# A tuned attention and feed-forward kernel: its first phase issued in another hand-listed order

## The chip, the cores and the metric

The kernel runs on one core of one Trainium2 chip. The metric is the device time of one execution in microseconds (us). Three runs of the kernel before gave 1009.29, 1008.87 and 1005.37 us; their median is 1008.87 us.

## The reference

The reference is a pooled attention whose output goes through a gated feed-forward layer. It is float32 throughout.

```python
k_p = k.reshape(B, H, Sp, 8, D).mean(axis=3)          # B=8, H=8, S=576, D=64, Sp=72
v_p = v.reshape(B, H, Sp, 8, D).mean(axis=3)
scores = q @ k_p.T / sqrt(D)
attn = softmax(scores)
x = (attn @ v_p) as 4608 tokens x 512
xn = x / sqrt(mean(x * x) + 1e-6) * rms_g
out = (silu(xn @ w_gate) * (xn @ w_val)) @ w_out      # 512 -> 1536 -> 512
```

## The kernel before, in words

The kernel has nine token blocks of 512 tokens. A first phase (`ORDER`, run by `first_phase`) computes the attention of batches 0 and 1, converts all weights from float64 words to pairs of float32r parts, and runs the feed-forward layer of block 0. A later phase (`LATER`) does the rest and is not changed. Within a phase the whole order of work is written out by hand: `ORDER` is a list of steps, `run` calls them one after another, and each engine executes its own instructions in just that order. An engine that waits therefore holds everything that stands behind it in its own list. GpSimd (POOL) and the queue of SyncE (SP), which issues all transfers, are kept in order in the same way.

A step is a letter with indices (base 36); after a colon stand the PSUM banks that it takes. The ones that matter here:

- For batch b and head pair p: `k`, `q`, `v` load (L361, L369, L380, on SP); `K` and `V` pool by eight on VectorE (L389, L398); `S` makes the scores on TensorE (L441). For each head h: `M` row maxima on VectorE (L407, L408), `E` exponentials on ScalarE (L419), `R` inverse sums on VectorE (L425, L426), `N` normalises on GpSimd (L431, tile prob for batch 1, main for batch 0). `T` transposes on TensorE (L501), `C` and `D` copy the result out by VectorE or ScalarE (L507, L509), `A` multiplies by the pooled v (L523), `Y`, `X` copy (L545), `Z`, `Q` square on ScalarE (L550, L560, L567), `J` joins the squares on GpSimd (L574, L576), `P` sums them on TensorE (L616), `p` adds two parts on VectorE (L621), `r` is a square root on ScalarE (L628), `s` its inverse on VectorE (L631), `B` spreads it on TensorE (L640), `I` scales block 0 on VectorE (L1008), `H` scales the rest.
- For weight chunk n of 26: `l` loads it (L290, SP), `a` takes the magnitude on ScalarE (L301), `b`, `c`, `d` put the bits together on VectorE (L305, L309, L313), `h` rounds on ScalarE (L327), `w` takes the remainder on VectorE (L331). Chunks 0 and 1 belong to slice 0 of the first layer, 2 to slice 1, 3 to slice 0 of the second layer, then alternately the first layer and the second.
- For slice f of 12 of block 0: `x`, `y` round the input and take its remainder (L1013 ScalarE, L1018 VectorE), `g` and `e` are the two products of the first layer, 12 matmuls each (L1029, tile psg), `G` is the silu on ScalarE (L1036), `F` the product with e on VectorE (L1041), `i` and `j` round and take the remainder (L1051, L1059), `o` is the product of the second layer, 12 matmuls (L1073, tile po). All `g` share bank 2 and all `e` bank 3.
- `z` with a count: so many products of the identity with itself, which nothing reads (`warm`, L1145). Each appears in the trace as two matmul records.

`ORDER` ends with the rounding of the next block's input (`t`) and the two last products `oa`, `ob`. Two more lists give the buffers out of which tiles are taken in turn: `OUTS` (two buffers, for the magnitudes of the second layer's chunks among others) and `STAGES` (four buffers, for loads and squares).

The lines that place the steps in engines are these:

```python
N=lambda b, p, h: s_norm(b, p, h, G), T=s_pt,
g=lambda f: mm1(0, f, 0), e=lambda f: mm1(0, f, 1), G=lambda f: gate(0, f), F=lambda f: val(0, f),
z=warm, t=lambda c: (x_hi(1, c), x_lo(1, c)))
nc.sync.dma_start(gcol, gain)
run(ORDER, 1, steps)
```

Of the kernel before, what the change touches and what calls it, by code (L numbers as in the profile page):

```python
# [49 lines left out]


ORDER = """
zg:0 k01 q00 k00 v00 K00 S00:01 K01 q01 v01 z1:7 S01:45 q02 k02 v03 v02 k03 q03 l3 M000 E000 l1 l0 V00 M010 M011 E011
l2 l5 k10 q10 R000 N000 M001 E001 K02 zf:7 S02:06 E010 T000:5 R011 N011 T011:1 V03 M020 E020 K03 z1:7 S03:32 R001 M021
E021 N001 T002:0 C011 M030 R020 N020 E030 C000 T001:1 C001 D002 M031 E031 R030 R021 N021 z4:7 T020:4 C020 V02 N030
R010 N010 z1:7 A001:0 Z01 Y001 R031 N031 A000:1 Z00 V01 a1 b1 c1 z1:7 T021:5 T022:0 D022 Y000 D021 a0 b0 T030:4 D030
A020:1 Z20 Y020 T010:0 D010 a2 c0 d0 z2:7 T012:1 C012 d1 A021:0 Z21 T031:4 C031 K10 T032:5 C032 Y021 h1 w1 h0 w0
A010:1 Z10 Y010 A011:0 Z11 l4 S10:46 M100 b2 M101 Y011 a5 b5 c2 A030:5 Z30 A031:0 J02 J01 a3 b3 Z31 z2:2 P01:7 za:2
P03 p X030 E100 R100 c3 E101 R101 N101 d3 r0 s0 zd:2 B00:1 Y031 N100 z2:2 T100:0 v10 V10 a4 b4 k11 K11 I2 l6 q11 v11
D100 I0 I1 I3 a6 b6 z3:2 T102:0 D102 T101:5 D101 B01:4 A100:0 x0 y0 x1 y1 x2 y2 Y100 x3 y3 h3 w3 A101:1 Y101 g0:2 e0:3  # L60
G0 d2 h2 c6 c5 l7 a7 w2 d6 h6 F0 i0 c4 b7 d4 h4 H01 j0 c7 S11:01 M111 d7 g1:2 e1:3 h7 G1 w4 d5 F1 o0:4567 g2:2 Q10 w7
h5 w5 i1 j1 l9 a9 lb l8 la ld a8 w6 b9 c9 ab bb M110 cb b8 d9 db G2 E110 R110 N110 o1 e2:3 g3:2 c8 F2 h9 E111 R111 V11
k12 w9 K12 d8 v12 lc q12 aa i2 j2 ba T110:0 D110 ad bd h8 w8 N111 T111:1 D111 ca cd da T112:0 D112 G3 e3:3 o2 g4:2 F3
dd ac bc cc hb hd wd wb A110:1 A111:0 Y110 i3 j3 Y111 e4:3 lf af bf V12 cf G4 ha wa o3 g5:2 lh le k13 F4 ae i4 dc j4
o4 v13 df ah bh be ce K13 de ch hc wc e5:3 G5 F5 dh he we lj lg li S12:01 M121 i5 M120 j5 q13 ll lm ag bg hh wh cg dg
hf ai bi wf aj bj cj g6:2 G6 e6:3 F6 o5 dj g7:2 e7:3 E121 R121 N121 E120 al i6 j6 bl hj wj hg Q11 R120 N120 cl J11
T121:0 C121 G7 F7 wg ci di T120:1 D120 T122:0 D122 lk ln ak bk o6 ck dl i7 am j7 A121:1 X121 V13 bm A120:0 Y120 hi wi
hl g8:2 G8 o7 Q12 J12 S13:01 M130 wl M131 dk E130 cm R130 E131 R131 an bn cn hk e8:3 F8 g9:2 dn hn wn i8 j8 N131
T131:0 D131 N130 T130:1 C130 e9:3 o8 T132:0 G9 dm hm D132 F9 i9 wk ga:2 A130:0 wm X130 A131:1 X131 lp ap lo ao bo Q13
j9 bp ea:3 o9 Ga cp dp Fa ia hp k20 v20 K20 ja co do J13 P10:0 r1 s1 gb:2 B10:0 H10 B11:1 Gb ho H11 eb:3 wo oa Fb ib  # L70
jb wp t2 t0 t3 t1 V20 ob q20
"""


# [138 lines left out]
dp7621 dp7631 dp7641 dp7651 do741 de741  # L213
"""
OUTS = """
0101110110010110010101010101010101010101010010101010101010101010101010101010101010101010101010101010101010101010
"""

DEEP = (7,)
# [3 lines left out]
HM = DM // 2  # L223

STAGES = """
0123023102310232131203103213231201233102131221302121032130213231031323132113210302330113003210203210320120323013031201
0130232121023101010231032132102103021302301
"""
EXP_SCALE = 1.0 / (POOL * float(np.sqrt(D)))
# [952 lines left out]
```

## Time and profile before

| what | value |
|---|---|
| median of three runs | 1008.87 us (1005.37 to 1009.29) |
| the profiled execution's own time | 1004.35 us |
| its span, first to last instruction | 1002.6 us |
| TensorE busy | 970.5 us (97%) |
| VectorE busy | 699.2 us (70%) |
| ScalarE busy | 492.8 us (49%) |
| GpSimd busy | 302.6 us (30%) |
| mean granted TensorE clock | 0.995 |

The profile is of one execution. Busy shares are means over the span; the first phase takes its first 176 us, where the shares are others. In the timelines a row gives the start, the duration, the engine, the line, the operation and its tiles, and in brackets the idle time of the engine before it with the work that ended that idle time. Matmul records overlap, so a group of 12 of them shows some 2.9 us in a row of its own and 2.72 us in the chain of waits, which counts from the end of the one before.

### The profile page before, as it was taken

How to read it: one execution, taken by the hardware profiler on the slowest of the kernel's cores; microseconds unless marked ns; L12 is line 12 of the kernel's file. 1: busy time of each engine (PE TensorE's matmuls, PEld its weight loads, DVE VectorE, ACT ScalarE, POOL GpSimd, SP SyncE). 2: the span in 40 equal slices, each digit the busy share in tenths (PEclk: the TensorE clock that was granted, in tenths of full speed). 3: DMA queues.
4: the chain of work that ended last, by engine and by line, in shares of the span. 5: the costliest groups of instructions: out<-in, count | busy, mean ns of one | idle time of the engine just before them, and what ended most of it. 6: DMA issues, size and time to landing. Idle time of an engine off the chain costs nothing.

```text
span 1002.6 us, 14211 instructions
## 1 busy us (share of the span) xinstructions
PE 970.5 (97%) x4832; PEld 764.5 (76%) x4832; DVE 699.2 (70%) x1131; ACT 492.8 (49%) x907; POOL 302.6 (30%) x285
## 2 busy tenths in 40 slices
PE   8996999999999999899999999999999999999998
PEld 7774867767677778787777878777788787888876
DVE  6996987775776857657778788876644655445565
ACT  5874765565556545344665464764222432223232
POOL 2303022376544678300111023155432001113330
PEclk9998999999999999999999999999999999999999
DMA  9534521677867772467777662777676606666665
GB/s 304 167 132 163 211 63 37 219 228 244 248 192 220 222 222 77 158 212 213 221 213 222 192 205 67 226 222 237 204 215 211 220 25 206 193 195 189 187 186 186
DMA packets 130200, 189.40 MB, mean 189 GB/s; under 512 B 10896, under 2 KB 76944, under 8 KB 128848
## 3 DMA queue, kind: packets, MB, share of 16 engines
q1 hardware_dynamic: 130128, 188.49, 61.1%
q8 instruction: 39, 0.64, 0.3%
q14 instruction: 33, 0.27, 0.1%
HBM read 132.22 MB, written 56.23 MB: 188 GB/s over the span
## 4 chain that ended last, share of the span: by engine, by line
PE 77%; DVE 9%; ACT 5%; DMA 3%; POOL 3%; issue 3%; SPq 1%; ACTq 0%; DVEq 0%; POOLq 0%
PE py L829 19%; PE po L1073 18%; PE px L829 14%; PE psg L1029 12%; PE pd L964 6%; PE psx L523 3%; PE pss L441 3%; POOL prob L431 1%; DVE hl L1059 1%; DMA main<-kT 1%; DMA out<-o 1%; DVE xraw L607 1%; ACT prob L419 1%; DVE w L331 1%; DVE act L1041 1%
## 5 line engine op out<-in xcount | busy, mean ns | idle before, releaser
L829 PE MATMUL py<-xp,wp 128*128 128x512 f32 x864 | 222.0, 392 | 0.9 <-DVE u L1137 0.8
L829 PEld LDWEIGHTS py<-xp,wp 128*128 128x128 f32 x864 | 160.6, 188 | 39.1 <-DVE u L1137 4.0
L1029 PE MATMUL psg<-xh,w 128*128 128x512 f32 x576 | 183.1, 400 | 3.5 <-DVE act L1041 3.0
L1073 PE MATMUL po<-w,hh 128*128 128x512 f32 x672 | 174.6, 390 | 0.0
L829 PE MATMUL px<-xp,wp 128*128 128x512 f32 x648 | 166.7, 393 | 2.2 <-ACT act L1132 2.2
L1073 PEld LDWEIGHTS po<-w,hh 128*128 128x128 f32 x672 | 126.0, 188 | 27.4 <-issue 0.8
L829 PEld LDWEIGHTS px<-xp,wp 128*128 128x128 f32 x648 | 120.3, 188 | 32.8 <-ACT act L1132 3.2
L1029 PEld LDWEIGHTS psg<-xh,w 128*128 128x128 f32 x576 | 106.6, 190 | 34.1 <-issue 6.7
L1029 PE MATMUL psg<-xl,w 128*128 128x512 f32 x288 | 112.6, 393 | 0.0
L472 POOL TENSOR_TENSOR prob<-prob,sm 128x360 f32<-128x360 f32 x48 | 40.8, 850 | 231.6 <-DVE sm L468 188.7
L1073 PE MATMUL po<-w,hl 128*128 128x512 f32 x336 | 97.4, 399 | 3.9 <-DVE hl L1059 3.6
L1073 PEld LDWEIGHTS po<-w,hl 128*128 128x128 f32 x336 | 61.2, 188 | 23.5 <-DVE hl L1059 7.5
L1130 ACT COPY hb<-px 128x512 f32<-128x512 f32 x36 | 21.2, 588 | 93.2 <-PE px L829 93.1
L1133 DVE TENSOR_TENSOR u<-u,py 128x512 f32<-128x512 f32 x36 | 24.7, 686 | 59.6 <-PE py L829 59.6
L1135 ACT ACTIVATE hb<-hb 128x512 f32<-128x512 f32 x36 | 22.7, 632 | 83.6 <-DVE hb L1134 83.4
L1029 PEld LDWEIGHTS psg<-xl,w 128*128 128x128 f32 x288 | 54.6, 189 | 12.0
L1059 DVE TENSOR_TENSOR hl<-act,hh 128x512 fp32r<-128x512 f32 x60 | 48.4, 807 | 20.7 <-ACT hh L1051 18.6
L964 PE MATMUL pd<-dp,wq 128*128 128x512 f32 x252 | 61.2, 390 | 0.3 <-DVE dp L937 0.3
L1051 ACT CAST hh<-act 128x512 fp32r<-128x512 f32 x60 | 37.3, 622 | 48.7 <-DVE act L1041 28.8
L964 PEld LDWEIGHTS pd<-dp,wq 128*128 128x128 f32 x252 | 47.2, 188 | 10.5 <-DVE dp L937 0.7
L738 POOL TENSOR_TENSOR wsum<-wsum 128x256 f32<-128x256 f32 x48 | 48.7, 1014 | 1.4
L462 ACT ACT_TABLE_LOAD x38 | 48.8, 1283 | 0.7
(160 smaller groups left out, 1506.0 us busy)
## 6 DMA issues: line engine op xcount, KB each, us to landing
wp<-sum SPq DMA_DIRECT2D x144, 256.0 KB
wp<-blocks SPq DMA_DIRECT2D x108, 256.0 KB
sum<-wt SPq DMA_DIRECT2D x48, 256.0 KB
blocks<-w SPq DMA_DIRECT2D x24, 512.0 KB
wx<-w SPq DMA_DIRECT2D x10, 1024.0 KB
v<-vN SPq DMA_DIRECT2D x32, 288.0 KB
wx<-w SPq DMA_DIRECT2D x16, 512.0 KB
k<-kT SPq DMA_DIRECT2D x28, 288.0 KB
```

The source lines that it names most:

```text
L441: nc.tensor.matmul(s["ps", h][:, t * SP:(t + 1) * SP], s["q"][r, o:o + P], s["pk"][r, :], start=True, stop=True)
L462: nc.scalar.activation(l_pr(h), l_pr(h), AF.Exp, scale=EXP_SCALE)
L472: nc.gpsimd.tensor_tensor(l_pr(h), l_pr(h), sm[:, :, None].broadcast_to([P, len(OFFS2), SP]), ALU.mult)
L523: nc.tensor.matmul(ps[r, :n], s["pv"][:, r], x, start=True, stop=True)
L738: nc.gpsimd.tensor_sub(place(f, y), place(f, a), place(f, b))
L829: nc.tensor.matmul(ps[:, :NB], w[:, a, c, :], x[:, b, c, :], start=j == 0 and not more, stop=j == len(todo) - 1, skip_group_check=more)
L964: nc.tensor.matmul(ps[:, :NB], w[:, a, c * P:(c + 1) * P], x[b], start=g == 0 and j == 0 and not more, stop=g == HF - 1 and j == 2, skip_g ...
L1029: nc.tensor.matmul(ps[:, :NB], w[:, c, cols], x[c], start=(j == 0), stop=(j == len(todo) - 1))
L1051: nc.scalar.copy(a, act_in(i, f))
L1059: eng.tensor_sub(l, act_in(i, f), hh[i, f].bitcast(F32))
L1073: nc.tensor.matmul(po[i, t], x[i, f][:, t * P:(t + 1) * P], w, start=(f == 0 and k == 0), stop=(f == NF - 1 and k == 2))
L1133: u3=lambda i, f: V.tensor_add(u3(i), u2(i), st["Y", i, f, 3]),
```

## The change

The list `ORDER` is replaced by another one. It holds the same steps, each on the same engine and with the same banks; the steps `z` alone differ in their counts. Of these, the first (16 products) stays, and the rest have 46 products where there were 55. Among the moves:

- `E101` stands behind `r0` and `s0`, where it stood before `r0`.
- `A100`, `A101` and `B01` stand behind `g0 e0`, where they stood ahead of `g0`; `V10` and `b4` stand behind `y3`.
- `G2` stands behind `E110` and `E111`, where it stood ahead of both.
- `T111` and `T110` stand behind `e3 o2`; they stood behind `g3`, ahead of `e3`. `N110` and `N111` are issued around `w6 db c8`.
- `A110` and `A111` stand ahead of `o3`, `J11` and `J12` behind `N130`, and `r1` ahead of `Ga`.

`OUTS` and `STAGES` change in a few places to go with it.

```diff
--- before.py
+++ after.py
@@ -50,25 +50,25 @@
 
 
 ORDER = """
-zg:0 k01 q00 k00 v00 K00 S00:01 K01 q01 v01 z1:7 S01:45 q02 k02 v03 v02 k03 q03 l3 M000 E000 l1 l0 V00 M010 M011 E011
-l2 l5 k10 q10 R000 N000 M001 E001 K02 zf:7 S02:06 E010 T000:5 R011 N011 T011:1 V03 M020 E020 K03 z1:7 S03:32 R001 M021
-E021 N001 T002:0 C011 M030 R020 N020 E030 C000 T001:1 C001 D002 M031 E031 R030 R021 N021 z4:7 T020:4 C020 V02 N030
-R010 N010 z1:7 A001:0 Z01 Y001 R031 N031 A000:1 Z00 V01 a1 b1 c1 z1:7 T021:5 T022:0 D022 Y000 D021 a0 b0 T030:4 D030
-A020:1 Z20 Y020 T010:0 D010 a2 c0 d0 z2:7 T012:1 C012 d1 A021:0 Z21 T031:4 C031 K10 T032:5 C032 Y021 h1 w1 h0 w0
-A010:1 Z10 Y010 A011:0 Z11 l4 S10:46 M100 b2 M101 Y011 a5 b5 c2 A030:5 Z30 A031:0 J02 J01 a3 b3 Z31 z2:2 P01:7 za:2
-P03 p X030 E100 R100 c3 E101 R101 N101 d3 r0 s0 zd:2 B00:1 Y031 N100 z2:2 T100:0 v10 V10 a4 b4 k11 K11 I2 l6 q11 v11
-D100 I0 I1 I3 a6 b6 z3:2 T102:0 D102 T101:5 D101 B01:4 A100:0 x0 y0 x1 y1 x2 y2 Y100 x3 y3 h3 w3 A101:1 Y101 g0:2 e0:3
-G0 d2 h2 c6 c5 l7 a7 w2 d6 h6 F0 i0 c4 b7 d4 h4 H01 j0 c7 S11:01 M111 d7 g1:2 e1:3 h7 G1 w4 d5 F1 o0:4567 g2:2 Q10 w7
-h5 w5 i1 j1 l9 a9 lb l8 la ld a8 w6 b9 c9 ab bb M110 cb b8 d9 db G2 E110 R110 N110 o1 e2:3 g3:2 c8 F2 h9 E111 R111 V11
-k12 w9 K12 d8 v12 lc q12 aa i2 j2 ba T110:0 D110 ad bd h8 w8 N111 T111:1 D111 ca cd da T112:0 D112 G3 e3:3 o2 g4:2 F3
-dd ac bc cc hb hd wd wb A110:1 A111:0 Y110 i3 j3 Y111 e4:3 lf af bf V12 cf G4 ha wa o3 g5:2 lh le k13 F4 ae i4 dc j4
-o4 v13 df ah bh be ce K13 de ch hc wc e5:3 G5 F5 dh he we lj lg li S12:01 M121 i5 M120 j5 q13 ll lm ag bg hh wh cg dg
-hf ai bi wf aj bj cj g6:2 G6 e6:3 F6 o5 dj g7:2 e7:3 E121 R121 N121 E120 al i6 j6 bl hj wj hg Q11 R120 N120 cl J11
-T121:0 C121 G7 F7 wg ci di T120:1 D120 T122:0 D122 lk ln ak bk o6 ck dl i7 am j7 A121:1 X121 V13 bm A120:0 Y120 hi wi
-hl g8:2 G8 o7 Q12 J12 S13:01 M130 wl M131 dk E130 cm R130 E131 R131 an bn cn hk e8:3 F8 g9:2 dn hn wn i8 j8 N131
-T131:0 D131 N130 T130:1 C130 e9:3 o8 T132:0 G9 dm hm D132 F9 i9 wk ga:2 A130:0 wm X130 A131:1 X131 lp ap lo ao bo Q13
-j9 bp ea:3 o9 Ga cp dp Fa ia hp k20 v20 K20 ja co do J13 P10:0 r1 s1 gb:2 B10:0 H10 B11:1 Gb ho H11 eb:3 wo oa Fb ib
-jb wp t2 t0 t3 t1 V20 ob q20
+k01 zg:0 q00 k00 K01 v00 q01 v01 q02 k02 v03 K00 V00 S00:01 M000 E000 M001 v02 k03 q03 l3 l1 l0 z1:7 S01:45 M010 M011
+E011 E001 K02 za:7 S02:06 R000 N000 T000:5 R011 N011 T011:1 M020 E020 R001 N001 z3:7 T002:0 V03 K03 S03:32 l2 l5 k10
+M021 C011 E010 R010 N010 R020 N020 M030 T001:1 C001 E021 C000 R021 N021 z4:7 T020:4 V01 V02 D002 A001:0 E030 R030 C020
+M031 Y001 Z01 A000:1 Z00 Y000 a1 b1 z1:7 T022:0 D022 a0 b0 c1 d1 T021:5 D021 T010:0 N030 T030:4 E031 R031 D010 A020:1
+Y020 Z20 c0 d0 D030 z3:7 A021:0 Z21 Y021 T012:1 C012 h1 h0 N031 T031:4 C031 K10 A011:0 Z11 A010:1 Z10 J02 w1 T032:5
+C032 q10 S10:46 M100 l4 v10 k11 l6 Y011 a2 b2 a3 b3 c2 Y010 c3 M101 A030:5 Z30 A031:0 Y031 Z31 J01 z2:2 P01:7 z8:2 P03
+p d3 E100 R100 N100 r0 s0 z9:2 B00:1 E101 z2:2 T100:0 D100 d2 X030 I0 h3 I3 R101 N101 z3:2 T102:0 w0 x0 T101:5 a5 I1
+I2 x1 x2 b5 y0 y1 y2 x3 y3 g0:2 e0:3 V10 a4 b4 D102 D101 A100:0 h2 w2 B01:4 c5 G0 F0 c4 i0 d5 H01 w3 q11 v11 l7 a7 l9
+lb d4 b7 j0 c7 h4 w4 h5 w5 d7 K11 g1:2 e1:3 a6 b6 G1 F1 A101:1 o0:4567 Y100 ab Y101 h7 w7 c6 i1 j1 a9 l8 a8 S11:01
+M111 M110 bb d6 cb E110 b8 R110 N110 h6 w6 db c8 E111 R111 N111 b9 g2:2 G2 o1 e2:3 F2 hb wb d8 V11 la ld k12 v12 i2 lc
+q12 lf ad bd lh j2 cd c9 d9 dd g3:2 G3 e3:3 o2 aa ba F3 h8 w8 V12 K12 ca da T111:1 T110:0 D111 h9 ac bc g4:2 e4:3 hd
+i3 j3 D110 wd T112:0 G4 D112 A110:1 A111:0 w9 F4 ha wa o3 g5:2 cc dc i4 ah af bf j4 o4 e5:3 cf df le k13 v13 lj lg ae
+hf bh wf be ce hc Y111 wc G5 de aj Y110 ag S12:01 ch bj M121 E121 bg M120 F5 cj dh R121 N121 i5 j5 cg he we E120 dg dj
+R120 g6:2 G6 e6:3 o5 g7:2 hj F6 wj i6 j6 hh wh T121:0 C121 li q13 ai ll lm al Q11 am lk bi bl cl dl ci V13 hg N120
+T120:1 D120 T122:0 D122 G7 e7:3 wg o6 g8:2 hl F7 A121:1 A120:0 wl bm cm K13 i7 Q10 j7 o7 ln lp an bn di cn dn ak bk
+X121 ck G8 Y120 S13:01 M130 M131 hi wi E130 R130 dk E131 R131 N131 N130 hk hn dm J11 Q12 J12 e8:3 F8 g9:2 i8 j8 T131:0
+D131 hm wm G9 wn T130:1 lo k20 ap wk C130 bp cp ao dp bo co do T132:0 D132 e9:3 F9 i9 o8 A130:0 X130 A131:1 X131 Q13
+J13 ga:2 ea:3 P10:0 r1 j9 o9 Ga Fa s1 ia gb:2 hp wp ja B10:0 ho wo B11:1 H10 H11 eb:3 oa Gb Fb ib jb t0 t2 t3 t1 K20
+v20 q20 V20 ob
 """
 
 
@@ -213,7 +213,7 @@
 dp7621 dp7631 dp7641 dp7651 do741 de741
 """
 OUTS = """
-0101110110010110010101010101010101010101010010101010101010101010101010101010101010101010101010101010101010101010
+0101010110001010101001010101010101010101010010101010101010101010101010101010101010101010101010101010101010101010
 """
 
 DEEP = (7,)
@@ -223,7 +223,7 @@
 HM = DM // 2
 
 STAGES = """
-0123023102310232131203103213231201233102131221302121032130213231031323132113210302330113003210203210320120323013031201
+0123013210302132021320303213231201233102131221302121032130213231031323132113210302330113003210203210320120323013031201
 0130232121023101010231032132102103021302301
 """
 EXP_SCALE = 1.0 / (POOL * float(np.sqrt(D)))
```

## Rows read from the trace of the kernel before

**Rows 1.** The page: TensorE's granted clock in 40 slices of 25 us

```profile
PEclk9998999999999999999999999999999999999999
```

**Rows 2.** Windows: stretch, its us, busy us of each engine, clock, DMA

```profile
48.24:74.60 26.36, 26.36 (x131) 21.38 (x131) 25.56 (x42) 19.02 (x44) 1.58 (x1) 1.00 0.36 133
...
48.24:176.03 127.79, 115.58 (x571) 91.29 (x570) 107.06 (x163) 78.05 (x164) 23.50 (x11) 0.97 0.34 120
```

**Rows 3.** Timeline of TensorE: transposes that waited for GpSimd

```profile
84.42 1.50 PE L501 MATMUL pst<-ident,prob 128*72 128x128 f32 x6 [9.34 <-POOL prob L431]
...
144.80 0.63 PE L501 MATMUL pst<-ident,prob 128*72 128x128 f32 x4 [1.35 <-POOL prob L431]
146.00 0.63 PE L501 MATMUL pst<-ident,prob 128*72 128x128 f32 x4 [0.56 <-POOL prob L431]
```

**Rows 4.** Timeline of GpSimd in the first phase

```profile
41.22 2.86 POOL L431 TENSOR_TENSOR prob<-prob,mx 128x360 f32<-128x360 f32 x2 [6.60 <-DVE mx L426]
...
74.83 9.54 POOL L431 TENSOR_TENSOR prob<-prob,mx 128x360 f32<-128x360 f32 x1 [0.43 <-DVE mx L426]
121.71 0.79 POOL L431 TENSOR_TENSOR prob<-prob,mx 128x360 f32<-128x360 f32 x1 [37.34 <-ACT wt L301]
...
143.67 2.27 POOL L431 TENSOR_TENSOR prob<-prob,mx 128x360 f32<-128x360 f32 x2 [5.48 <-ACT wt L301]
...
159.35 2.72 POOL L729 TENSOR_TENSOR wsum<-w 128x1024 f32<-128x1024 f32 x1
```

**Rows 5.** Timeline of VectorE, around two of those

```profile
74.60 1.18 DVE L398 TENSOR_REDUCE pv<-v 72x128 f32<-72x1024 f32 x1
...
82.50 1.22 DVE L313 SCALAR_TENSOR_TENSOR wt<-wx,wt 128x1024 uint32<-128x1024 uint32 x1
...
89.42 0.69 DVE L1041 TENSOR_TENSOR act<-act,psg 128x512 f32<-128x512 f32 x1 [5.71 <-PE psg L1029]
90.03 0.69 DVE L313 SCALAR_TENSOR_TENSOR wt<-wx,wt 128x512 uint32<-128x512 uint32 x1
...
159.86 2.76 DVE L313 SCALAR_TENSOR_TENSOR wt<-wx,wt 128x512 uint32<-128x512 uint32 x1
```

**Rows 6.** Windows of 10 us, with the columns of rows 2

```profile
80.00:90.00 10.00, 5.58 (x22) 4.62 (x23) 4.29 (x5) 4.15 (x6) 4.37 (x1) 0.66 0.87 357
```

**Rows 7.** The chain that ended last: start, us, what

```profile
70.60 1.63 ACT prob L419 x10
...
85.92 3.40 PE psg L1029 x12
...
92.04 2.72 PE psg L1029 x12
...
136.52 1.32 PE pss L441 x20
```

**Rows 8.** Timeline of TensorE, up to the first product of block 0

```profile
35.93 2.48 PE L1145 MATMUL warm<-ident 128*128 128x128 f32 x20
...
39.19 3.15 PE L1145 MATMUL warm<-ident 128*128 128x128 f32 x26
42.17 1.22 PE L640 MATMUL psb<-ident,r 116*128 116x116 f32 x10
...
46.12 0.33 PE L640 MATMUL psb<-ident,r 116*128 116x64 f32 x2
46.64 1.67 PE L523 MATMUL psx<-pt,pv 72*64 72x288 f32 x8 [0.19 <-ACT pt L509]
48.24 2.12 PE L1029 MATMUL psg<-xh,w 128*128 128x512 f32 x8
```

**Rows 9.** Timeline of VectorE ahead of that product

```profile
44.02 2.71 DVE L1008 SCALAR_TENSOR_TENSOR xraw<-xraw,gcol,psb 128x512 f32<-128x512 f32 x4
...
47.62 2.55 DVE L1018 TENSOR_TENSOR xl<-xraw,xh 128x512 fp32r<-128x512 f32 x4 [0.30 <-ACT xh L1013]
```

**Rows 10.** Timeline of ScalarE there: the table load of the square root

```profile
38.40 1.28 ACT L628 ACT_TABLE_LOAD   x1
```

## The prediction

> **What bounds the kernel now.** I read the span first: TensorE is busy for most of it, so the question is where in the first phase, which alone changes, TensorE stands still. The windows come next. From the first product of block 0 at 48.24 us to the phase's last product at 176.03 lie 127.79 us, of which TensorE is busy 115.58 and VectorE 107.06 [rows 2]. In the part up to 74.60 TensorE has no idle time at all and VectorE next to none, 25.56 of 26.36 us. So this stretch is bound by TensorE, with VectorE close behind.
>
> Then the timeline of TensorE: of the 12.2 us that it loses, 9.34 are one wait at 84.42, of the transposes T111 for GpSimd; 1.35 and 0.56 are later waits of the same kind [rows 3]. GpSimd's timeline shows what it was: the norm N111 begins at 74.83 and takes 9.54 us [rows 4], where a norm with nothing in its way takes 0.79. VectorE's timeline gives the reason: from 74.60 to 83.72 it runs without a gap, and the norm ends 0.65 us after that run [rows 5]. TensorE stood still meanwhile, with its next product behind T111, and its clock was granted at 0.66 in the window from 80 to 90 us, so for a part of it at 1.2 and not 2.4 GHz [rows 6]. VectorE in turn had to wait 5.71 us afterwards for a product [rows 5]. What stands before 48.24 us is a chain of latencies, where TensorE fills its time with unread products [rows 8].
>
> **The change, part by part.** The work is the same; only its places and 9 products fewer.
>
> *The wait for N111.* In the new list R111 and N111 come some 26 us after the first product, and between the scores S11 and T111 stand g2, o1, e2, g3, e3 and o2. Six groups at 2.72 us [rows 7] are 16.3 us, where g2, o1, e2, g3 gave 10.9. The cover counts from when N111 can begin, and at the latest it is let in at F3, whose operand comes from PSUM and which follows e3; o2 still runs then, for 2.72 us, and a norm takes 0.79. So the wait goes: -9.34. With it goes the slow clock: the product group after it took 3.40 us in the chain, the next like it 2.72 [rows 7], so 0.7, and half again for the transposes: -1.0.
>
> *Ahead of the first product.* The fillers between the last attention products and B00 shrink: 20 and 26 records took 2.48 and 3.15 us [rows 8], and 16 and 18 will take 2.0 and 2.2, together 1.45 less. The square root can follow, because E101 (1.5 us) no longer stands before it on ScalarE. E101 then pays a table load that it did not pay before, 1.28 [rows 10]; its user is T101, not the chain of the root. B00 ended at 43.39, so will at 41.9. VectorE began the four scalings I at 44.02 and ended y3 at 50.17 [rows 9]; V10 and b4 no longer stand before the scalings but after y3, and R101, w0 and b5 come in between, half a microsecond more than stood there. The end of y3, which the first product's last part waits for, comes at about 48.2: -2.0. Bounds: 0, if E101's inverse sum R101 is late, and +5, if N101 is late (below).
>
> *Moved behind it.* A100, A101 and B01 now run behind the first product: 0.33 and 1.67 us [rows 8], 2.0 more that TensorE does after it: +2.0. It was part of the time before 48.24 and its going is in the -2.0 above.
>
> *New waits.* The norms of the last pair keep their waits of 1.35 and 0.56 [rows 3]: S13, e8, g9 and T131 stand as they stood. G2 now stands behind E110, a weight cast and E111. In the last pair the first norm began at 143.67 [rows 4], 5.8 us after the scores' end at 137.84 [rows 7]; with the cast and a second table load it is some 8.5 until G2 ends, and g3 needs its bank. The cover is g2, o1, e2, 8.2 us. Between 0 and +1.5; I take +0.6, for the row of the norm is the nearest. J11 and J12 now run back to back behind N130. A GpSimd operation that has begun keeps VectorE out: a 512-column operation beside the 2.72 us sum of weights took 2.76 us [rows 4, 5] and 0.69 without [rows 5]. The loss was 2.07 for 1024 columns; a join has 576, so 1.2 each by an estimate from those rows. F9 stands behind that run and frees bank 3 for ea. Between 0 and +2.4; I take half, +1.2.
>
> *Queues.* SP: v11 waits until V10 has freed its buffer, and l7, l9 and lb queue behind it; V10 comes later by 6 us, and so do these loads. Their first user a7 stands on ScalarE behind G0 and i0, which wait for g0 and e0: cost 0, and 2 if the load lands after that. GpSimd: only norms and joins, dealt with. The buffers taken in turn: a7 now follows w3's release, but h4 behind it waits for d4 at about that time anyway: 0, at most 1.
>
> *The sum.* -9.34 - 1.0 - 2.0 + 2.0 + 0.6 + 1.2 = -8.5 us. The later phase begins with products of the next block that follow without a gap, so the phase's gain is carried to the end. The profiled execution took 1004.35 us, which gives 995.8. That execution lies 4.5 below the median of the runs; against 1008.87 the forecast is **1000.3 us**.
>
> *A rule against the rows.* Row first: N111 began 0.2 us into V11, a reduction of 1.18 us from 74.60 on, and was not done with it; it was held for the whole run [rows 4, 5]. The Trainium skill ("SBUF — State Buffer", section "Who interferes with whom") says that a reduction never contends with GpSimd, and that whichever operation starts first has the shared ports for its whole length. By that N111 would have begun inside V11 and been done at 75.6; its 9.54 us would have another cause, which another order may cover but does not take away, and the sum would be that of the third rival in place of -8.5. The measurement decides: for the reduction the trace does not agree. It does on the second half, in the 2.76 us above.
>
> **The rivals.** *VectorE becomes the bound.* The 9.34 us were VectorE's lead: it worked through them, and then waited 5.71 us and more for TensorE [rows 5]. Without it, 107 us of VectorE work and the moved V10 and b4 meet some 119 us instead of 127.79, and each weight part comes just in time. For it: 25.56 of 26.36 us in the part before the wait [rows 2]. Against it: in that part TensorE lost nothing. If half of the lead was needed, +4.5: 1004.8 us.
>
> *N101 is held.* R101 is followed on VectorE by w0, I1, I2, b5, the four y, V10, b4, w2 and c5 without a wait of which I am sure, and T102 and T101 stand ahead of the first product. The norms at 41.22 came through beside other work [rows 4], but no row shows a norm that begins beside a scaling I. If N101 is let in only at the end of that run, the ten operations at 0.65 us (a quarter of the I or y row [rows 9]) and more for the longer ones give +7: 1007.3 us.
>
> *The norm's 9.54 us are its own.* The hold may come back with N111 wherever it stands, whatever VectorE does: then it ends 9.5 us after R111, some 36 us after the first product, against T111 at 34.5 or so. Its price is +1.4: 1001.7 us. For it: the reduction in rows 5 as the Trainium skill reads it ("SBUF — State Buffer"). Against it: the norms in rows 4 that took no more than 1.4 us each, and the end of this one, right after VectorE's run.
>
> *The clock falls early: slower than before.* With 9 products fewer the fall to 1.2 GHz that came in TensorE's long idle time [rows 6] may come ahead of the first product, in the stretch that these products fill. From 35.93 us to the end of e0 TensorE has some 14 us of its own in a row; at half the clock they take twice that: +14, so 1014.3 us. It decides from the point where more than 8.5 us of products run at half. Against it: the granted clock is full in every slice up to the wait but the first [rows 1], and the fillers that remain are the longest of them.
>
> *The later waits vanish too*, G2's, the joins' and those of the last pair: another -0.6 - 1.2 - 1.9, so 996.6 us.
>
> **How the numbers follow.** Forecast 0.55; VectorE the bound 0.20; N101 held 0.10; the later waits vanish 0.05; the norm's own time 0.06; the clock 0.04. Below 0.5% (about 5 us) a measurement of this kernel can't tell a change from none, so faster by more than that means below 1003.8 us: nearly all of the forecast (0.52), a third of VectorE's case (0.07), the better case and the norm's own (0.11) make 0.70. Within it: the rest of those and N101, 0.25. Slower: the clock and what of N101 goes with a fallen clock, 0.05. The range runs from 993, where the better case meets runs as far below the median as the profiled one, to 1007.5, where N101's case begins to end; the forecast alone has bounds of 997 and 1004.
>
> **What would show it.** Right: T111 without a wait of more than 1 us; first product at 46 and last at about 168 us; granted clock full through the first 170 us; the transposes T131 and T130 still waiting nearly 2 us. Each step wrong: if TensorE waits at g or o for a remainder w or j, VectorE is the bound; if T101 waits for GpSimd and the first product comes after 50 us, it was N101; if a window ahead of it shows a granted clock below 1, it was the clock; if N111 takes 9 us with VectorE idle in it, the cause of the old wait was not VectorE. The forecast as a whole is wrong if the first phase's last product does not come at least 5 us earlier than 176.03, or if it does and the later phase gives it back.

## The result, and the profile after

The changed kernel takes 995.23 us (median of four runs, 993.60 to 996.81), the kernel before on the same chip 1007.71 (four runs, 1005.37 to 1009.29): ratio 0.9878, 95% interval [0.985, 0.9905], so 1.2% faster, with the whole interval below 1. The two profiled executions differ by less: 1004.35 us before and 995.29 after, 9.06. The other 3.4 us are in the runs that were not profiled (below).

Of the span's 9.1 us (1002.6 to 993.5), 2.13 come ahead of block 0's first product (48.24 to 46.11 us), 6.19 between it and the phase's last product, and 0.78 later. First the page of the kernel after: span, busy time and granted clock.

```profile
span 993.5 us, 14189 instructions
...
PE 968.0 (97%) x4814; PEld 761.3 (77%) x4814; DVE 697.1 (70%) x1131; ACT 494.1 (50%) x908; POOL 290.3 (29%) x285
...
PEclk9999999999999999999999999999999999999999
```

GpSimd is busy 12.3 us less with the same work, as the page counts a held operation as busy. The dip of the clock in the fourth slice [rows 1] is gone. Next, windows after, with the columns of [rows 2]: first to last product, and ten microseconds where the stall had been [rows 6].

```profile
46.11:167.71 121.60, 117.37 (x581) 90.95 (x578) 108.60 (x168) 80.94 (x168) 13.12 (x11) 1.00 0.40 137
...
80.00:90.00 10.00, 9.85 (x52) 7.37 (x50) 9.96 (x14) 6.00 (x11) 0.00 (x0) 1.00 0.74 266
```

Between first and last product TensorE is now idle for 121.60 - 117.37 = 4.23 us, where it was 127.79 - 115.58 = 12.21 [rows 2]: 7.98 less. It is busy for 1.79 more; A100, A101 and B01, which now stand in the stretch, are the largest part of that. VectorE is busy for 108.60 of the 121.60 us.

TensorE's timeline after: T102's wait ahead of the first product, that product with the part that takes the remainders y, the scores S11, then the waits that are left, with T111 and T110 (at 81.98) among them.

```profile
45.61 0.74 PE L501 MATMUL pst<-ident,prob 128*72 128x128 f32 x5 [1.10 <-POOL prob L431]
46.11 2.10 PE L1029 MATMUL psg<-xh,w 128*128 128x512 f32 x8
48.05 1.47 PE L1029 MATMUL psg<-xl,w 128*128 128x512 f32 x4
...
62.32 1.34 PE L441 MATMUL pss<-pk,q 64*128 64x72 f32 x20
...
73.68 0.74 PE L1029 MATMUL psg<-xh,w 128*128 128x512 f32 x2 [1.64 <-ACT act L1036]
...
81.98 1.03 PE L501 MATMUL pst<-ident,prob 128*72 128x128 f32 x8
...
111.56 0.73 PE L1029 MATMUL psg<-xh,w 128*128 128x512 f32 x2 [0.34 <-ACT act L1036]
116.10 0.41 PE L501 MATMUL pst<-ident,prob 128*72 128x128 f32 x2 [0.62 <-DVE pt L507]
137.31 1.38 PE L501 MATMUL pst<-ident,prob 128*72 128x128 f32 x8 [1.09 <-POOL prob L431]
```

There is no wait at T111. The largest behind the first product is g3's, for G2 on ScalarE, 1.64 us; T131 waits 1.09 in place of 1.35. GpSimd after, with N111 in the first row and the two joins in the last:

```profile
73.94 0.79 POOL L431 TENSOR_TENSOR prob<-prob,mx 128x360 f32<-128x360 f32 x1 [3.29 <-DVE mx L426]
136.21 1.79 POOL L431 TENSOR_TENSOR prob<-prob,mx 128x360 f32<-128x360 f32 x2 [22.51 <-DVE mx L426]
137.96 3.25 POOL L576 TENSOR_TENSOR acc<-acc,sq 128x576 f32<-128x576 f32 x2
```

And VectorE beside them, again after:

```profile
73.69 0.39 DVE L305 TENSOR_SCALAR wt<-wt 128x512 uint32<-128x512 uint32 x1
73.99 0.68 DVE L1041 TENSOR_TENSOR act<-act,psg 128x512 f32<-128x512 f32 x1
74.59 0.69 DVE L331 TENSOR_TENSOR w<-wt,w 128x512 fp32r<-128x512 f32 x1
...
138.35 1.57 DVE L1059 TENSOR_TENSOR hl<-act,hh 128x512 fp32r<-128x512 f32 x1 [1.15 <-ACT hh L1051]
139.84 2.52 DVE L331 TENSOR_TENSOR w<-wt,w 128x512 fp32r<-128x512 f32 x2
```

The norm N111, 9.54 us before [rows 4], takes 0.79: it becomes ready 0.25 us into db (L305), runs beside that and F2, whose operand is in PSUM, and ends about when the next remainder begins (74.73 and 74.59). VectorE goes on without a gap. The two joins stretch j8 to 1.57 us, where such an operation takes 0.68 elsewhere, and the two weight remainders behind it to 2.52 together, where two take some 1.29.

### The profile page after: what moved, and what is told of

It is laid out like the page before. It is cut to its first block, busy times and chain, and to the rows that moved or that the text cites. A ratio compares the mean times of both kernels' runs of the same rounds, so it can differ in the third digit from the quotient of the medians.

```text
span 993.5 us, 14189 instructions
## 1 busy us (share of the span) xinstructions
PE 968.0 (97%) x4814; PEld 761.3 (77%) x4814; DVE 697.1 (70%) x1131; ACT 494.1 (50%) x908; POOL 290.3 (29%) x285
## 4 chain that ended last, share of the span: by engine, by line
PE 77%; DVE 12%; ACT 3%; issue 3%; DMA 2%; POOL 1%; SPq 1%; ACTq 0%; DVEq 0%; POOLq 0%
PE py L829 19%; PE po L1073 19%; PE px L829 14%; PE psg L1029 12%; PE pd L964 6%; PE pss L441 3%; PE psx L523 3%; DVE w L331 1%; DVE hl L1059 1%; DVE wt L309 1%; DVE wt L313 1%; DMA main<-qT 1%; DVE xraw L607 1%; DVE pv L398 1%; POOL wsum L738 1%
## 5 line engine op out<-in xcount | busy, mean ns | idle before, releaser
L1059 DVE TENSOR_TENSOR hl<-act,hh 128x512 fp32r<-128x512 f32 x60 | 50.4, 841 | 18.6 <-ACT hh L1051 16.8
L751 POOL TENSOR_TENSOR wt<-wsum,wt 128x256 fp32r<-128x256 f32 x48 | 37.9, 794 | 36.0 <-ACT wt L747 36.0
```

The costliest lines, as they stand in the source:

```text
L751: nc.gpsimd.tensor_sub(y[:, 1], place(f, f"T{k}"), y[:, 0].bitcast(F32))
L1059: eng.tensor_sub(l, act_in(i, f), hh[i, f].bitcast(F32))
```

## The experiments

**1. The cover alone** (`e1`): in the old list T110, T111 and T112 move behind e3 and o2, where the new one has T111 and T110. The lines of the lists are shown in part; "..." marks what is left out.

```diff
-... aa i2 j2 ba T110:0 D110 ad bd h8 w8 N111 T111:1 D111 ca cd da T112:0 D112 G3 e3:3 o2 g4:2 F3
+... aa i2 j2 ba ad bd h8 w8 N111 ca cd da G3 e3:3 o2 T110:0 D110 T111:1 D111 T112:0 D112 g4:2 F3
```

> The kernel before, with the transposes T110, T111 and T112 moved behind e3 and o2 on TensorE and nothing else. If the cover alone takes the stall away (my theory), no transpose waits over 1 us, the clock is full through the first phase, the phase's last product ends at 176.0 - 9.3 - 1.0 = 165.7 us plus at most 2 us of waits for VectorE, which lost its lead: 166 to 168, ratio 0.990. If VectorE needed the lead (rival), products g4 to g6 wait for remainders and the end comes after 170 us. If the norm's 9.5 us are its own (rival), N111 still ends near 84 us, and the time is as for the first theory.

Measured: 999.92 us (997.82 to 1003.08), ratio 0.992 [0.9891, 0.9949]. The timeline of GpSimd in `e1`, N111:

```profile
75.56 9.54 POOL L431 TENSOR_TENSOR prob<-prob,mx 128x360 f32<-128x360 f32 x1 [0.43 <-DVE mx L426]
```

VectorE's in `e1`, F3:

```profile
84.37 0.68 DVE L1041 TENSOR_TENSOR act<-act,psg 128x512 f32<-128x512 f32 x1
```

And TensorE's in `e1`, o2 and T111:

```profile
79.55 1.20 PE L1073 MATMUL po<-w,hl 128*128 128x512 f32 x4 [1.41 <-DVE hl L1059]
...
85.15 1.27 PE L501 MATMUL pst<-ident,prob 128*72 128x128 f32 x6 [2.12 <-POOL prob L431]
```

N111 is held as long as before, and by its end it came in beside F3; T111 waits 2.12 us for it, and o2 1.41 for its remainder. The phase's last product ends at 171.89 us, not at 166 to 168, and the clock is at half for 3.4 us near 22 and for 3.4 near 87. So the cover hides most of the stall, and leaves it where it was.

**2 and 3. Which operation lets the norm in.** In the old list either F2, with its PSUM operand, is put behind the inverse sum R111 (`e2`), or only K12 and w9 change places, so that behind the reduction V11 stands a second reduction and not a remainder, which has two inputs in SBUF (`e3`). `e3` was timed again in `e12`.

```diff
-... g3:2 c8 F2 h9 E111 R111 V11 ...     (e2)
+... g3:2 c8 h9 E111 R111 F2 V11 ...
-... R111 V11 k12 w9 K12 d8 ...          (e3, e12)
+... R111 V11 k12 K12 w9 d8 ...
```

> The kernel before, with one VectorE operation moved: F2, which takes an operand from PSUM, stands behind R111 in place of ahead of it. If the norm is held by VectorE's run and let in beside an operation with a PSUM operand (my theory), N111 ends by 76 us, T111 waits under 1 us in place of 9.34, and the phase ends near 167 to 168 us. If the 9.5 us are the norm's own, N111 takes 9 us again and T111 waits as before.

> The kernel before, with K12 moved ahead of w9, so that two reductions from SBUF (V11, K12: 1.9 us together) follow R111 directly. If reductions let GpSimd in, as the Trainium skill says (SBUF - State Buffer, Who interferes with whom), N111 ends by 76.5 us and T111 waits about 1 us. If a waiting norm comes in only where VectorE pauses or has a PSUM operand, N111 is held until 83 to 84 us again and T111 waits about 9.3 us.

> The list before with the one move of e3 (K12 ahead of w9), timed, since e3 was a single execution. Theory A: the new list earns its gain in two places, the wait of 9.34 us at T111 with the clock lost behind it, and 2.1 us ahead of the first product; the one move takes the first alone, with 1 to 2 us more between first product and last since A100, A101 and B01 stay ahead of g0. Then T111 waits under 1 us, first product 48 to 49 us, some 118 to 120 us from there to the phase's last product, time 995 to 999, ratio 0.987 to 0.991. Theory B: the new list gains by its whole order, and the stall comes back or other waits grow with the one move: T111 waits over 5 us or the stretch takes over 122 us, time 1001 or more, ratio over 0.993.

Measured: `e2`, one execution, 1001.95 us, T111 waits 0.59; its first product came late, at 53.45 us behind a fall of the clock at 36, and so the phase ended at 172.70, not at 167 to 168. N111 in `e2`, on GpSimd, and F2 and V11 on VectorE:

```profile
80.02 0.79 POOL L431 TENSOR_TENSOR prob<-prob,mx 128x360 f32<-128x360 f32 x1 [0.43 <-DVE mx L426]
```

```profile
79.79 0.65 DVE L1041 TENSOR_TENSOR act<-act,psg 128x512 f32<-128x512 f32 x1
80.35 1.21 DVE L398 TENSOR_REDUCE pv<-v 72x128 f32<-72x1024 f32 x1
```

So the 9.54 us are not the norm's own. Since a reduction stands behind F2 here, `e2` does not tell by which of the two the norm came in.

`e3`, one execution, 995.83 us; `e12`, six runs, 996.86 us (994.92 to 999.47), ratio 0.9883 [0.986, 0.9906]. The timeline of GpSimd in `e3`, N111:

```profile
78.00 0.79 POOL L431 TENSOR_TENSOR prob<-prob,mx 128x360 f32<-128x360 f32 x1 [0.43 <-DVE mx L426]
```

VectorE's in `e3`, V11 and what follows it:

```profile
77.77 1.18 DVE L398 TENSOR_REDUCE pv<-v 72x128 f32<-72x1024 f32 x1
78.86 0.74 DVE L389 TENSOR_REDUCE pk<-k 128x72 f32<-128x576 f32 x1
79.52 0.68 DVE L331 TENSOR_TENSOR w<-wt,w 128x512 fp32r<-128x512 f32 x1
```

And TensorE's in `e3`, T111:

```profile
78.84 1.02 PE L501 MATMUL pst<-ident,prob 128*72 128x128 f32 x6 [0.59 <-POOL prob L431]
```

The norm starts 0.23 us into V11, as it did before [rows 4, 5], and is done inside it; `e12` has the same 0.79 and 0.59 us. In the kernel before, V11 was followed by the remainder w9 and then by K12:

```profile
75.70 0.68 DVE L331 TENSOR_TENSOR w<-wt,w 128x512 fp32r<-128x512 f32 x1
76.30 0.74 DVE L389 TENSOR_REDUCE pk<-k 128x72 f32<-128x576 f32 x1
```

Two tokens of the old list exchanged remove the stall. In `e12` the time from first to last product is 120.2 us (50.54 to 170.76), in `e3` 118.4, where before had 127.8; in `e12` the first product came late behind a fall of the clock at 33.7 us. Its interval overlaps the changed kernel's: one exchange gives most of the 1.2%, and these runs can't tell the two kernels apart.

**4 and 5. Both kernels again, unchanged** (`e4` before, `e5` after; no edit).

> The kernel before, unchanged. The profiled execution of before lies 1 to 5 us below its other runs. If the stall of N111 differs from run to run, this profile shows a wait of T111 that is clearly not 9.3 us; if it is fixed, the wait is 9.2 to 9.5 us again and the spread comes from elsewhere (the later phase or the granted clock).

> The changed kernel, unchanged, for the clock of many runs. My theory for what the medians gained beyond the two profiles (12.5 us against 9.1) is that before loses TensorE's full clock ahead of the first product in most of its runs, and the changed kernel does not. Then nearly all runs here show a mean granted clock of 0.995 or more and 993 to 998 us, where before shows 0.984 to 0.995. If the changed kernel loses it as often, the clocks spread down to 0.99 and the median is near 999.

Measured: `e4` 1009.69 us (1006.12 to 1015.24, ten runs), ratio 1.0017 [0.9992, 1.0041]; `e5` 994.40 (994.19 to 999.99, five runs), ratio 0.986 [0.983, 0.9889]. Five runs of `e5` had mean granted clocks of 0.994 to 1.000, the fifteen of before beside them 0.986 to 0.993. The profiled execution of `e4` happens to be its slowest, 1015.24 us. Its windows of 10 us:

```profile
30.00:40.00 10.00, 9.31 (x69) 7.09 (x68) 8.91 (x17) 9.24 (x35) 3.46 (x2) 0.81 0.48 175
...
80.00:90.00 10.00, 0.90 (x5) 0.78 (x6) 8.40 (x11) 2.66 (x4) 9.05 (x1) 0.70 0.71 253
90.00:100.00 10.00, 10.00 (x38) 8.09 (x37) 4.32 (x6) 4.79 (x7) 0.00 (x0) 0.79 0.37 150
...
150.00:160.00 10.00, 8.85 (x37) 7.02 (x37) 7.19 (x10) 4.63 (x9) 1.72 (x2) 0.83 0.15 53
...
265.00:275.00 10.00, 7.10 (x22) 4.71 (x20) 7.88 (x15) 5.10 (x8) 4.76 (x6) 0.66 0.61 201
```

The stall is the same (T111 waits 9.33 us), but behind it the clock stays at half until 94 us, where TensorE is busy without a pause, and it also falls near 36, 152, 268 and 436 us. The profiled execution of before spent 6.8 us at half clock behind the stall and 3.4 near 261; this one spent 30.6 there in five places.

**6. Is the early fall the cause?** (`e6`) In the old list eight more unread products cover the scores S03, which waited 2.18 us in `e4` up to 19.59 us, some 16 us ahead of the fall at 36.

```diff
-... E020 K03 z1:7 S03:32 ...
+... E020 K03 z9:7 S03:32 ...
```

> The kernel before, with 9 unread products in place of 1 ahead of S03, where TensorE waits 1.4 to 2.3 us for the load of k03. By my theory (the clock falls after that wait in many runs) the wait is filled, the clock stays full up to 80 us in the profile, the mean clocks of the runs rise to 0.990 to 0.995 and the median falls by 2 to 4 us, with T111 waiting 9.3 us as before. If that wait is not what makes the clock fall, clocks and median stay (0.984 to 0.995, 1007 us).

Measured: 1008.52 us (1004.46 to 1011.37), ratio 0.9988 [0.9969, 1.0007], mean clocks 0.988 to 0.995. In the profile the clock was full until the stall, and fell there for 10.2 us and near 149 and 265 for 3.4 each. S03 did not wait, and the median came 0.57 us lower where 2 to 4 were expected; the interval leaves room for up to 3.1. So the wait at S03 is not shown to cost the runs of before their clock, and what the early fall costs them stays open. Such a fall came in the profiles of `e1`, `e2`, `e3` and `e12` too (from 20, 36, 20 and 33 us on), which all have the old list's opening, and in none of the seven with the new one. `e12` narrows it down all the same: with that opening kept and the stall gone, its six runs have clocks of 0.994 to 1.000, and the eleven of before beside them 0.987 to 0.993.

**7 and 9. g3's wait** (`e7`, `e9`). In the new list the gate G2 goes ahead of the exponentials E110 and E111 (`e7`), or the row maxima M111 and M110, and E111 with them, go ahead of the weight work (`e9`).

```diff
-M111 M110 bb d6 cb E110 b8 R110 N110 h6 w6 db c8 E111 R111 N111 b9 g2:2 G2 o1 e2:3 F2 ...
+M111 M110 bb d6 cb g2:2 G2 h6 E110 b8 w6 db E111 R110 N110 c8 R111 N111 b9 o1 e2:3 F2 ...   (e7)
-... c6 i1 j1 a9 l8 a8 S11:01 M111 M110 bb d6 cb E110 b8 R110 N110 h6 w6 db c8 E111 R111 N111 ...
+... i1 a9 l8 a8 S11:01 M111 M110 j1 c6 bb d6 cb E110 E111 b8 R110 N110 h6 w6 db R111 N111 c8 ...   (e9)
```

> The changed kernel, with the gate G2 put ahead of E110 and E111 again (and w6, R110 moved to follow h6 and E110). In the changed kernel g3 waits 1.64 us for G2's bank. If that wait is G2's place behind both exponentials, it goes and the phase's last product comes 1 to 1.6 us earlier, at about 166.3. If VectorE is the bound behind it (rival), the wait moves to o2 or g4, for j2 or w8, and the end stays at 167.5 to 168.

> The changed kernel with M111 and M110 ahead of j1 and c6 on VectorE, and E111 ahead of h6 on ScalarE, so that both exponentials and G2 come some 1.3 us earlier. In the changed kernel g3 waits 1.65 us for G2; putting G2 first (e7) only moved the wait to e3 and o2, because VectorE came later. If this order frees G2 without delaying VectorE (theory), g3 waits under 0.5 us, o2 under 0.5, and the phase ends 1.0 to 1.6 us earlier counted from the first product (120.0 to 120.6 in place of 121.6). If VectorE is the bound anyway (rival), the wait returns at o2 or g4 and the count stays at 121 to 122.

Measured: `e7` 996.37 us, ratio 0.9861 [0.9835, 0.9887]; `e9` 996.26, ratio 0.9871 [0.9846, 0.9895]. TensorE's timeline in `e7`:

```profile
74.16 0.73 PE L1029 MATMUL psg<-xh,w 128*128 128x512 f32 x2 [0.36 <-DVE act L1041]
...
77.96 1.19 PE L1073 MATMUL po<-w,hl 128*128 128x512 f32 x4 [0.79 <-DVE hl L1059]
...
83.43 0.50 PE L1029 MATMUL psg<-xh,w 128*128 128x512 f32 x1 [1.01 <-DVE w L331]
```

And in `e9`:

```profile
72.14 0.72 PE L1029 MATMUL psg<-xh,w 128*128 128x512 f32 x2 [0.57 <-ACT act L1036]
...
78.84 1.20 PE L1073 MATMUL po<-w,hl 128*128 128x512 f32 x4 [0.78 <-DVE hl L1059]
...
83.71 0.50 PE L1029 MATMUL psg<-xh,w 128*128 128x512 f32 x1 [0.73 <-DVE w L331]
```

g3's wait is gone or down to 0.57 us, and comes back at e3 (`e7`), o2 and g4, as waits for VectorE's product F2 and its remainders; first to last product take 122.6 and 122.4 us, where `e5` had 121.6. Here VectorE is the bound, and what ScalarE wins is not passed on.

**8 and 10. Fewer fillers** (`e8`), and these with `e9`'s edit (`e10`).

```diff
-... z2:2 P01:7 z8:2 P03 p d3 E100 R100 N100 r0 s0 z9:2 B00:1 ...
+... z2:2 P01:7 z4:2 P03 p d3 E100 R100 N100 r0 s0 z4:2 B00:1 ...
```

> The changed kernel, with 4 unread products in place of 8 ahead of P03 and 4 in place of 9 ahead of B00. If the fillers stand on the chain to the first product (my reading), P03 and B00 come 1.0 us earlier and so do y3 and the end of the phase, 166.7 us. If the clock needs them (rival), the profile or the mean clocks of the runs show a fall ahead of the first product and the median is 2 us or more above that of the changed kernel.

> e9 and the cut fillers of e8 together. The first product comes 1.0 us earlier, as in e8, where g3 gave 0.6 of it back; if g3 is freed as in e9, the phase ends near 164.5 to 165.5 us in the profile and the ratio to before falls to 0.982. If the clock falls behind the shorter fillers (e8 showed one fall at 72 us), the gain is lost again and the median is as for e8.

Measured: `e8` 994.00 us (993.30 to 994.98), ratio 0.9838 [0.9808, 0.9868]; `e10` 993.61 (992.86 to 994.76), ratio 0.9844 [0.9822, 0.9867]. In `e8` the first product comes at 44.15 us, 1.0 before `e5`'s, and g3 waits 2.24 in place of 1.65. But the phase's last product ends at 167.29, where `e5` had 166.74 and 166.7 was expected: from first to last it is 123.1 us. The clock fell at 72 us, behind g3's wait, as this window of `e8` shows:

```profile
70.00:80.00 10.00, 7.76 (x28) 6.23 (x28) 9.93 (x17) 6.64 (x11) 0.79 (x1) 0.83 0.54 199
```

In `e10` the first product comes at 43.49 us, g3, o2 and g4 wait 0.75, 0.74 and 0.73, and the phase ends at 166.09, not at 164.5 to 165.5. Both medians are under the changed kernel's 994.40 and 995.23, but all these intervals overlap: faster than before is shown, faster than the changed kernel is not.

**11. The new list without its cover** (`e11`): T111 and T110 directly behind g3.

```diff
-... g3:2 G3 e3:3 o2 aa ba F3 h8 w8 V12 K12 ca da T111:1 T110:0 D111 ...
+... g3:2 G3 T111:1 T110:0 e3:3 o2 aa ba F3 h8 w8 V12 K12 ca da D111 ...
```

> The changed kernel with T111 and T110 put back to directly behind g3, ahead of e3 and o2, where before had them. If the norm no longer waits because F2 stands behind R111 on VectorE (what e2 shows), N111 still takes 0.8 us and T111 waits under 0.5 us: the longer cover was not needed and the time is that of the changed kernel. If the cover is what removed the stall (as the prediction put it), T111 waits several us.

Measured: one execution, 992.83 us; first to last product 121.6 us, as in `e5`. The timeline of GpSimd in `e11`:

```profile
72.26 0.79 POOL L431 TENSOR_TENSOR prob<-prob,mx 128x360 f32<-128x360 f32 x1 [3.29 <-DVE mx L426]
```

And TensorE's in `e11`, T111 and T110:

```profile
74.87 1.03 PE L501 MATMUL pst<-ident,prob 128*72 128x128 f32 x8
```

The transposes wait for nothing: N111 is done at 73.05 us, inside g3. The cover of e3 and o2, by which the forecast let the wait go, has nothing to hide in the new list.

## Why the prediction was right and wrong

**Right in what goes.** The wait of 9.34 us at T111 went (forecast -9.34), the first product came 2.13 us earlier (forecast -2.0), and the last product of the phase came 8.32 us earlier (forecast -8.5, at 168; it came at 167.71). The later phase kept the gain and added 0.78. The -2.0 is right in part by luck. The forecast took it from the end of y3, at 50.17 us before and expected at 48.2; y3 ended at 48.97, 1.20 earlier, and the four products that take it took 1.47 us in place of 1.07. The first product begins earlier because A100, A101 and B01 no longer stand ahead of it on TensorE, and what it follows now is T102, which waits 1.10 us for N101, and T101.

**Wrong in why.** The forecast let a longer cover hide the wait, 16.3 us in place of 10.9, and N111 be let in at F3. The 10.9 was misread: in the old list seven product groups, not four, stood between the scores S11 and T111 (g1, e1, o0, g2, o1, e2, g3), 19 us by the same 2.72 each. S11 itself moved, from 53.91 us to 62.32 behind o0. Its row before:

```profile
53.91 1.34 PE L441 MATMUL pss<-pk,q 64*128 64x72 f32 x20
```

What grew is only the part behind N111, by e3 and o2. `e11` takes the cover away and nothing waits; `e1` adds it to the old list and N111 is still held for 9.54 us. In the new list the norm is not held at all. The reading that fits is that F2 is next on VectorE when N111 becomes ready: the forecast's fallback, an operand from PSUM, one slice too late. `e1` agrees with F3, where the held norm came in, and `e2` with F2 in the old list, though there a reduction followed. No run takes F2 away from N111 in the new list, so for that list this step is argued and not shown. The number could not tell the two: in the changed kernel F3 begins at 81.53 us and T111 at 81.98, so a norm let in at F3 would have cost T111 some 0.3 us, by an estimate from these starts and the 0.79.

**The terms.** G2's wait was taken at +0.6 and measured 1.64, just beyond its bound of +1.5: G2 ended 9.97 us after the scores S11 (73.63 less 63.66), where 8.5 was estimated. The joins were taken at +1.2: VectorE paid (j8 took 1.57 us and the two remainders behind it 2.52, some 2.1 more than without the joins), and TensorE did not wait at ea, so the term was 0 at the end of the phase. T131 and T130 wait 1.21 together in place of 1.91. Unforeseen were 0.34 at g7 and 0.62 at T122. They nearly cancel.

**The term that failed** is the step from the profiled execution to the median: "That execution lies 4.5 below the median of the runs; against 1008.87 the forecast is 1000.3". Profile to profile the forecast of 995.8 is 0.5 from the 995.29 measured. But the 4.5 us did not carry over: the changed kernel's profiled execution lies at its median (995.29 and 995.23), and what the usual run of before lost beyond its profile went with the stall. In the runs of `e12`'s set the mean clock of before is 0.990, so TensorE was at 1.2 GHz for 2 x 0.010 x 1006 = some 20 us, against 2 x 0.005 x 1002.6 = 10 in the profiled execution; where TensorE is busy, 10 us more at half clock cost 5, by an estimate from these clocks. The changed kernel and `e12` stay at 0.994 to 1.000. So the -1.0 for the clock was read from an execution that lost little by it, and 3.4 us more (12.5 by the medians less 9.06 by the profiles) went with it in the usual run, so some -4.4. That removing the stall restores the clock is shown by `e12`; why the clock falls again near 150 and 265 us in some runs of before was not settled.

**The rivals.** *VectorE the bound* did not come about as a loss of 4.5 us, but it is what lies behind the wait that `e7` and `e9` remove. *N101 is held*: no; T102 waits 1.10 us for it, and it came in beside a scaling I. *The norm's 9.54 us are its own*: no, it takes 0.79 in `e2`, `e3`, `e11` and in the changed kernel, although T111 in `e11` stands where that rival would have paid. *The clock falls early*: not in the changed kernel's profiles; the old list's opening does it now and then (`e4`, and `e1`, `e2`, `e3` and `e12`). *The later waits vanish*: in part, the joins' and 0.7 of the last pair's.

**The rule against the rows.** The Trainium skill ("SBUF — State Buffer", section "Who interferes with whom") says that a reduction never contends with GpSimd. `e3` agrees: the norm ran inside V11, 0.79 us. The kernel before and `e1` do not: the same norm, 0.23 us into the same V11, was held. By the rule it would have ended at 74.83 + 0.79 = 75.62, before V11 did, so only what stood behind V11 differed, a remainder with two SBUF inputs. The rule tells of two operations that overlap, and here the third one, still queued, decided. Why it does is not shown by any run.

## What to carry to other kernels

Where a GpSimd operation shows a long span that begins beside VectorE's work, look first at the two or three VectorE instructions from the moment it becomes ready: one exchange (`e3`, `e12`) did nearly what a new list of the whole phase did. Ask of a stall what it costs in the usual run, clock included, and read that from several executions before an offset of one of them is carried over. And when VectorE is busy for 108.6 of 121.6 us, a wait that is freed on ScalarE can come back in the products behind it (`e7`, `e9`).

## What the hardware did that was not expected

- A norm that becomes ready inside a reduction is let in when another reduction follows (0.79 us, `e3`, `e12`) and held for 9.54 us when a remainder with two SBUF inputs follows (before, `e1`, `e4`, `e6`). Once held, it was not let in by the reduction K12 or by two operations with one input (L305, 1.02 us together) later in the same run of VectorE. With an operation with a PSUM operand next it came in although such a remainder followed (F2 in the changed kernel, 73.99 and 74.59).
- The opposite holds too: two joins of GpSimd, the first of which had begun, stretched j8 to 1.57 us, as the sum of weights did with another operation before [rows 4, 5].
- The same program ran with mean clocks from 0.984 to 0.995 and times from 1003.7 to 1015.24 us, while the program without the stall kept to 0.994 to 1.000. One profile of before could show no fall of the clock but the stall's and one more.
